# Routing attention and a squared-ReLU feed-forward on one core: narrow sums everywhere, last sums behind five products, one more pair turned by transfers, two heads in one load

## The chip, the cores and the metric

The kernel runs on one core of a Trainium2 chip. The metric is the device time of one execution in microseconds; the kernel before takes 984.49 us (median of 3 runs, 984.35 to 984.61). The profile shown is that of one execution with a span of 983.0 us.

The engines are called as in the profile: PE is TensorE (matmuls; PEld its weight loads), DVE is VectorE, ACT is ScalarE, POOL is GpSimd, SP is SyncE, whose queue (SPq) issues nearly all transfers here. L707 means line 707 of the kernel before.

## The reference

Four batches, eight heads, 768 rows of 64 numbers, 16 centroids per head; then a feed-forward on 3072 rows, 512 to 2048 to 512.

```python
q_assign = argmax(q_n @ c_n.T)          # cluster of each query, likewise k_assign
mask = q_assign[:, :, :, None] == k_assign[:, :, None, :]
scores = scale * np.matmul(q, k.transpose(0, 1, 3, 2))
scores = np.where(mask, scores, -1000000000.0)
attn = np.exp(scores - max)
attn = attn / (np.sum(attn, axis=-1, keepdims=True) + 1e-09)
out = np.matmul(attn, v)
# heads side by side: x is (3072, 512)
h = x @ w_in;  r = np.maximum(h, 0.0);  y = (r * r) @ w_out
```

So a key counts for a query only where both have the same nearest centroid; every query's weights are divided by their sum; and the result goes through two matrices with a squared ReLU in between.

## The kernel before

**Tiling.** The work goes by pairs of heads: pair = 4 * batch + hp, 16 pairs in all. The 768 queries of a pair are taken in two halves (h = 0, 1) of 384 columns (TB), the keys in six chunks of 128, two chunks at a time. One unit is (pair, h, c) with c = 0, 2, 4: 96 units. Batch 0 has its own order: units 0 to 11 are the first halves of pairs 0 to 3, units 12 to 23 their second halves. From unit 24 on (pairs 4 to 15) a pair does both halves, six units.

**A unit.** `scores` (L439) makes the products keys x queries into two PSUM tiles of two banks, ScalarE takes the exponential (L466). In batch 0 the mask is a second product of one-hot codes (`ohT`, bf16) added in PSUM; from batch 1 on VectorE multiplies with the mask instead (L470). `times_v` (L502) multiplies with v and accumulates in `av`. The exponentials also have to be summed over the keys. For the first halves of batch 0 (`first_half`) TensorE does it, by products with a tile of constants (`ups`), one for every unit, accumulated in `sm`. For all others GpSimd adds the exponentials up in `acc` (L480, L482), and a few products at the end of the half (L540) sum `acc` over the partitions.

**Sums.** `ones_products` (L486) has two forms. The narrow one writes 32 rows for 192 columns in each of four column groups; its result holds each sum once for a block of 32 rows. The reciprocal (L551) is then written to DRAM (`far_r`) and read back, repeated over 64 rows for each head (`rb`, L558). The wide form, used for pair 3's first half alone (`wide`, L498), writes 64 rows for 384 columns, so that the reciprocal (L545) is at once in the place of `rb`. `finish` (L567, profile line L570) multiplies `av` with `rb` into `xT`, the input of the feed-forward. Every reciprocal row also goes to `seen`, which is checked at the end.

**Before the scores.** Queries and keys must be turned, head dimension on the partitions. `load_qk` (L101) loads a pair, one transfer for each head of q and of k, into tiles where the two heads lie side by side (256 bytes each). For batch 0 `turn` (L249) transposes on TensorE, three parts of four, and ScalarE copies each part out (L258). For pairs 4 to 15 `split_words` (L269) copies the halves of each number apart on ScalarE (`flat`, L277, held by `issue_after` behind the last exponential traced), writes them to DRAM (`words`, L278), and `turn_words` (L286) reads them back with a transposing transfer (L288). Then come `logits` (L296, products with the centroids), `route` (L309: transposes L317, the argmax on VectorE L340 to L349) and the one-hot codes (`turn_onehot`, L363) or their spread (L394). `prep` (L409) lists these steps for a pair, and the main loop takes up to three of the list in each unit.

**Feed-forward.** The two halves of batch 0 are done plainly (`ffn`, L579: products L584 and L597), drawn in small portions between the units as filling for TensorE: `share` (L849 to L854) spreads the columns that are left over the units to come, RESERVE keeps three products of 512 columns for after the loop. A half enters the filling when `ends` (L784) has finished its last pair. The other three batches are done after the loop by `ffn_pair` (L610), which saves one product in eight (lines L676 and L707 in the profile).

**Weights.** In the first units 32 weight tiles are loaded (L139, four ahead), and each is rounded in six steps on ScalarE (L150, L152), VectorE (L155, L159, L162) and GpSimd (L166), four tiles in three units.

**Order.** The source is traced unit by unit. A scheduler then gives every engine its list: among the instructions that it reckons ready it takes the one traced first, where `high_priority` moves a block forward and `issue_after` holds one back. On the chip each engine works its list in order, and so does SyncE's queue. The loop delays things by hand: `complete` and `late` (L812 to L818) say in which unit `add_up` (L529) is traced after the last `times_v` of a half, `added` when `finish` follows.

Of the kernel before, what the change touches and what calls it, by code (L numbers as in the profile page):

```python
# [8 lines left out]
F32 = mybir.dt.float32  # L9
# [9 lines left out]
P = 128  # L19
# [6 lines left out]
def kernel(  # L26
# [74 lines left out]
    def load_qk(pair):  # L101
        if pair >= NG:
            return
        b, hp = divmod(pair, HP)
        raw[pair] = []
        for name, src in (("q_raw", q), ("k_raw", k)):
            t = loads.tile([P, NCH, 2 * D], F32, name=name, tag="qk")
            for e in range(2):
                (nc.scalar if pair == 0 and e else nc.sync).dma_start(
                    t[:, :, D * e : D * (e + 1)],  # L110
                    src[b, 2 * hp + e].rearrange("(p j) d -> p j d", p=P),
                )
            raw[pair].append(t)
# [135 lines left out]
    def turn(pair, part):  # L249
        if part == 0:  # L250
            pool = qkt_early if 2 <= pair < HP else qktp
            qkT[pair] = pool.tile([P, 2 * NCH, P], F32, name="qkT")
        pt = bank("pt", [P, 4, P])
        for i in range(4):
            which, c = divmod(4 * part + i, NCH)
            nc.tensor.transpose(out=pt[:, i], in_=raw[pair][which][:, c], identity=ident)
        dst = qkT[pair][:, 4 * part : 4 * part + 4]
        nc.scalar.copy(out=dst, in_=pt)  # L258
        if part == 2:
            raw.pop(pair)  # L260
            if pair in (0, 1, HP - 2):
                load_qk(pair + 2)


# [4 lines left out]
    def split_words(pair, which):  # L269
        if which == 0:  # L270
            words[pair] = dram.tile([2 * NCH, P, 2, 2 * D], U16, name="words")
        flat = loads.tile([P, NCH, 2, 2 * D], U16, name="flat", tag="qk")
        src = raw[pair][which].bitcast(U16).rearrange("p c (d two) -> p c two d", two=2)
        half = NCH // 2
        with tc.issue_after(last_exp[0]):
            for cols in (slice(0, half), slice(half, NCH)):
                nc.scalar.copy(out=flat[:, cols], in_=src[:, cols])  # L277
        nc.sync.dma_start(  # L278
            words[pair][NCH * which : NCH * (which + 1)].rearrange("c p two d -> p c two d"),
            flat,  # L280
        )
        if which == 1:
            raw.pop(pair)
            load_qk(pair + 1)

    def turn_words(pair):  # L286
        qkT[pair] = qktp.tile([P, 2 * NCH, P], F32, name="qkT")
        nc.sync.dma_start(  # L288
            qkT[pair].rearrange("p c n -> p (c n)").bitcast(U16),
            words.pop(pair).rearrange("c p two d -> (c p two) d"), transpose=True,  # L290
        )
# [17 lines left out]
    def route(pair):  # L309
        with tc.high_priority(offset=2000) if pair <= HP else ExitStack():  # L310
            number(pair)
# [95 lines left out]
        )  # L407

    def prep(pair):  # L409
        if pair < HP:  # L410
            return [
                lambda: turn(pair, 0), lambda: turn(pair, 1), lambda: turn(pair, 2),
                lambda: logits(pair), lambda: route(pair),
                lambda: turn_onehot(pair, 0), lambda: turn_onehot(pair, 1),
            ]

        split = [lambda i=i: split_words(pair + 1, i) for i in range(2 if pair + 1 < NG else 0)]
        first, second = split or (None, None)
        return [
            lambda: turn_words(pair), None, None, first, None, None,  # L420
            lambda: logits(pair), None, lambda: route(pair), second, None, None,
            None, None, lambda: spread(pair),
        ]
# [59 lines left out]
                out=acc[pair, h], in0=acc[pair, h], in1=t[:, 2 * i : 2 * i + 2], op=ALU.add  # L483
            )

    def ones_products(sm, wide, e, rhs, first, last):  # L486

        n = TB if wide else TB // 2
        rows = P * n // (2 * TB)
        return [  # L490
            dict(
                out=sm[rows * r : rows * (r + 1)], lhsT=ups[:, 0:rows],
                rhs=rhs[:, n * i : n * (i + 1)], start=first, stop=last,
            )
            for i, r in enumerate(range(e * P // (2 * rows), (e + 1) * P // (2 * rows)))
        ]

    def wide(pair, h):  # L498

        return (pair, h) == (HP - 1, 0)  # L500

    def times_v(pair, h, c):  # L502
        if c == 0:
            av[pair, h] = ps_av.tile([P, TB], F32, name="av", tag="av")
            if first_half(pair, h):
                n = TB if wide(pair, h) else TB // 2
                sums[pair, h] = ps_av.tile([P, n], F32, name="sm", tag="av")
        t = ex.pop((pair, h, c))
        products = [
            dict(  # L510
                out=av[pair, h][D * e : D * (e + 1)], lhsT=raw_v[pair][:, e, c + i],
                rhs=t[:, 2 * i + e], start=(c + i == 0), stop=(c + i == NCH - 1),
            )
            for i in range(2) for e in range(2)
        ]
        if first_half(pair, h):
            for i in range(2):
                one = [
                    ones_products(
                        sums[pair, h], wide(pair, h), e, t[:, 2 * i + e], c + i == 0, c + i == NCH - 1  # L520
                    )
                    for e in range(2)
                ]
                products += [p for both in zip(*one) for p in both]
        together(products, 4000)
# [3 lines left out]
    def add_up(pair, h):  # L529


        b, hp = divmod(pair, HP)
        if first_half(pair, h):
            sm = sums.pop((pair, h))
            if not wide(pair, h):
                nc.scalar.copy(out=xT_of(b, h)[:, hp], in_=av.pop((pair, h)))
        else:
            total = acc.pop((pair, h))
            sm = bank("sm", [P, TB // 2])
            one = [ones_products(sm, False, e, total[:, e], True, True) for e in range(2)]  # L540
            together([p for both in zip(*one) for p in both])
        row = 4 * (2 * pair + h)
        if wide(pair, h):
            rb = rbp.tile([P, TB], F32, name="rb")
            nc.vector.reciprocal(out=rb, in_=sm)  # L545
            nc.sync.dma_start(
                seen[row : row + 4], rb.rearrange("(e p) (g n) -> e p g n", e=2, g=2)[:, 0]
            )
        else:
            r = once.tile([P, TB // 2], F32, name="r")  # L550
            nc.vector.reciprocal(out=r, in_=sm)  # L551
            r = r.rearrange("(r p) n -> r p n", r=4)[:, 0]
            far = dram.tile([2, TB], F32, name="far_r")
            nc.sync.dma_start(far.rearrange("e (g n) -> (e g) n", g=2), r)
            nc.sync.dma_start(seen[row : row + 4], r)
            rb = rbp.tile([P, TB], F32, name="rb")
            for e in range(2):
                nc.sync.dma_start(rb[D * e : D * (e + 1)], far[e].partition_broadcast(D))  # L558
        spread_out[pair, h] = rb

    def xT_of(b, h):
        if (b, h) not in xT:
            pool = {0: xtp, 1: xt_first, 2 * B - 1: xtp}.get(2 * b + h) or later["xT"]
            xT[b, h] = pool.tile([P, KT, TB], F32, name="xT")
        return xT[b, h]
# [218 lines left out]
    def ends(halves):  # L784
        for pair, h in halves:
            b, hp = divmod(pair, HP)
            finish(pair, h)
            if hp == HP - 1 and (b, h) in PLAIN:
                fill.append(ffn(b, h))

    for u in range(len(units) + 2):
        if u < len(units):
            pair, h, c = units[u]
            if (p := next_pair(u)) is not None:
# [18 lines left out]
        while v_next < min(ready, len(units)):  # L813
            pair, h, c = units[v_next]
            times_v(pair, h, c)
            v_next += 1
            if c == NCH - 2:
                (late if u < HP * NCH and h else complete).append((pair, h))  # L818
        for pair, h in complete:
            with tc.high_priority(offset=1000) if first_half(pair, h) else ExitStack():  # L820
                add_up(pair, h)
            if h == 1:
                for d in (qkT, ids, qid):
                    d.pop(pair)
            if h == 1 or pair < HP:
                raw_v.pop(pair)
            if wide(pair, h):
                with tc.high_priority(offset=1000):
                    ends([(pair, h)])
            else:  # L830
                added.append((pair, h))

        rounding += 4
        while rounding >= 3:
# [263 lines left out]
```

## Time and profile before

| what | us |
|---|---|
| median time | 984.49 |
| span of the profiled execution | 983.0 |
| TensorE busy | 962.6 (98%) |
| VectorE busy | 562.4 (57%) |
| GpSimd busy | 376.9 (38%) |
| ScalarE busy | 315.4 (32%) |
| attention with plain feed-forward between | 0 to 543 |
| paired feed-forward (L676, L707) | 543 to 983 |
| scores and av products with their masks (L91, L94) | the greater part of 0 to 543 |
| plain feed-forward products L584 and L597 | 91.8 and 92.7 |

A line of the order in time reads: start in us, duration in us, engine, line and operation, what is written from what, shapes, how many; in brackets the idle time of the engine ahead of it and what ended it. In the chain of waits a line has start, duration and what the chain followed. A line of waits reads: who waited for whom, us in total, times, longest us. A line of SPq shows how long SyncE took to issue a transfer, not how long the transfer took.

### The profile page before, as it was taken

What the parts mean: (1) busy time and instruction counts of PE and PEld (TensorE: products, weight loads), DVE (VectorE), ACT (ScalarE), POOL (GpSimd) and SP (SyncE); (2) the same over time, 40 slices, a digit from 0 to 9 for tenths busy, and PEclk for the clock granted to TensorE, in tenths of its full rate; (3) what the DMA queues carried; (4) which work ended last, traced back from release to release, by engine and by line L of the source; (5) the groups of instructions that cost most, each with busy time, mean ns of one, the idle gap of its engine ahead of it and who ended that gap; (6) DMA issues with size and microseconds to landing.
All of it is one profiled execution on the core that took longest, in us unless ns stands there. A gap on an engine that the chain in (4) does not pass through costs nothing.

```text
span 983.0 us, 12011 instructions
## 1 busy us (share of the span) xinstructions
PE 962.6 (98%) x4455; PEld 552.8 (56%) x4455; DVE 562.4 (57%) x913; ACT 315.4 (32%) x510; POOL 376.9 (38%) x277
## 2 busy tenths in 40 slices
PE   7999989999999999999999999999999999999997
PEld 4544444443344444443343555888556888556886
DVE  5777778766566665667654865532566531656331
ACT  5886755444445545544231111000111000111000
POOL 1336666655656556565666231002231002231000
PEclk9999999999999999999999999999999999999999
DMA  9666572534546345452310000000000000000000
GB/s 248 199 186 177 164 212 76 136 108 106 135 111 156 98 109 123 111 142 75 74 42 16 15 0 1 11 22 22 11 1 1 21 22 22 1 0 1 22 22 24
DMA packets 127575, 74.32 MB, mean 76 GB/s; under 512 B 90906, under 2 KB 118934, under 8 KB 127510
## 3 DMA queue, kind: packets, MB, share of 16 engines
q1 hardware_dynamic: 125798, 73.06, 28.1%
q8 instruction: 37, 0.61, 0.3%
q10 hardware_dynamic: 1712, 0.43, 0.2%
q14 instruction: 28, 0.23, 0.1%
HBM read 48.07 MB, written 15.86 MB: 65 GB/s over the span
## 4 chain that ended last, share of the span: by engine, by line
PE 81%; DVE 6%; DMA 5%; issue 3%; ACT 1%; POOL 1%; SPq 1%; ACTq 0%; DVEq 0%; POOLq 0%
PE bank L707 22%; PE bank L676 22%; PE po L597 7%; PE ph L584 6%; PE sc L91 6%; PE sc L94 5%; PE av L91 5%; PE av L94 4%; DMA rb<-far_r 3%; DVE w_raw L162 1%; DVE r L551 1%; PE sm L91 1%; DVE ex L470 1%; DMA far_r<-r 1%; POOL w_in L166 1%
## 5 line engine op out<-in xcount | busy, mean ns | idle before, releaser
L482 POOL TENSOR_TENSOR acc<-acc,ex 128x768 f32<-128x768 f32 x112 | 207.1, 1849 | 115.0 <-DVE ex L470 98.4
L470 DVE SCALAR_TENSOR_TENSOR ex<-qid,ids,sc 128x384 f32<-128x384 bf16 x288 | 157.7, 608 | 63.3 <-ACT sc L466 45.6
L466 ACT ACTIVATE sc<-sc 128x768 f32<-128x768 f32 x144 | 108.5, 792 | 162.1 <-PE sc L94 144.6
L94 PE MATMUL sc<-qkT 64*128 64x384 f32 x576 | 153.4, 505 | 0.7
L94 PE MATMUL av<-ex,v_raw 128*64 128x384 f32 x576 | 136.9, 495 | 0.0
L665 POOL TENSOR_TENSOR w_s<-w_in 128x256 f32<-128x256 f32 x24 | 18.3, 762 | 279.9 <-PE bank L707 162.0
L646 DVE TENSOR_TENSOR g<-bank,g 128x384 f32<-128x384 f32 x144 | 77.9, 556 | 81.5 <-PE bank L676 80.5
L707 PE MATMUL bank<-w_out,g 128*128 128x256 f32 x432 | 95.2, 379 | 0.0
L584 PE MATMUL ph<-xT,w_in 128*128 128x384 f32 x256 | 91.8, 498 | 3.3 <-DVE best L341 2.3
L597 PE MATMUL po<-w_out,gT 128*128 128x512 f32 x192 | 92.7, 615 | 0.0
L91 PE MATMUL sc<-qkT 64*128 64x384 f32 x192 | 87.9, 538 | 2.6 <-DVE ex L470 2.6
L707 PEld LDWEIGHTS bank<-w_out,g 128*128 128x128 f32 x432 | 82.1, 190 | 11.8
L646 DVE TENSOR_TENSOR osb<-bank,osb 128x256 f32<-128x256 f32 x54 | 22.1, 423 | 107.6 <-PE bank L707 102.2
L94 PEld LDWEIGHTS sc<-qkT 64*128 64x128 f32 x576 | 65.4, 187 | 28.6 <-issue 6.7
L91 PE MATMUL av<-ex,v_raw 128*64 128x384 f32 x192 | 81.0, 504 | 0.0
L676 PE MATMUL bank<-xT,w_in 128*128 128x384 f32 x192 | 69.9, 487 | 0.0
L676 PE MATMUL bank<-x_t,w_s 128*128 128x384 f32 x192 | 69.8, 486 | 0.0
L676 PE MATMUL bank<-xT,w_s 128*128 128x384 f32 x192 | 69.8, 486 | 0.0
L584 PEld LDWEIGHTS ph<-xT,w_in 128*128 128x128 f32 x256 | 45.6, 189 | 42.7 <-issue 16.0
L94 PEld LDWEIGHTS av<-ex,v_raw 128*64 128x64 f32 x576 | 49.8, 137 | 34.6 <-issue 34.4
L480 POOL TENSOR_TENSOR acc<-ex 128x768 f32<-128x768 f32 x28 | 51.0, 1822 | 46.9 <-DVE ex L470 39.0
L707 PE MATMUL bank<-w_t,g_s 128*128 128x256 f32 x288 | 65.1, 379 | 0.0
(128 smaller groups left out, 1222.8 us busy)
## 6 DMA issues: line engine op xcount, KB each, us to landing
words<-flat SPq DMA_DIRECT2D x24, 384.0 KB
w_raw<-in_moe_w_in_dram SPq DMA_DIRECT2D x16, 512.0 KB
w_raw<-in_moe_w_out_dram SPq DMA_DIRECT2D x16, 512.0 KB
v_raw<-in_v_dram SPq DMA_DIRECT2D x20, 384.0 KB
q_raw<-in_q_dram SPq DMA_DIRECT2D x31, 192.0 KB
k_raw<-in_k_dram SPq DMA_DIRECT2D x31, 192.0 KB
rb<-far_r SPq DMA_DIRECT2D x62, 96.0 KB
out_dram<-osb SPq DMA_DIRECT2D x23, 256.0 KB
```

The source lines that it names most:

```text
L91: last = nc.tensor.matmul(**next(products))
L94: last = nc.tensor.matmul(**product)
L466: last_exp[0] = nc.scalar.activation(out=t[:, 2 * i : 2 * i + 2] if pair < HP else src, in_=src, func=ACT.Exp, scale=SCALE).ins
L470: nc.vector.scalar_tensor_tensor(out=t[:, 2 * i + e], in0=qid[pair][1][:, h, e], scalar=ids[pair][:, ch % NB, 2 + ch // NB, e : e + 1], in ...
L480: nc.gpsimd.tensor_tensor(out=acc[pair, h], in0=t[:, 0:2], in1=t[:, 2:4], op=ALU.add)
L482: nc.gpsimd.tensor_tensor(out=acc[pair, h], in0=acc[pair, h], in1=t[:, 2 * i : 2 * i + 2], op=ALU.add)
L584: nc.tensor.matmul(ph, lhsT=w_in[:, kk, f * P : (f + 1) * P], rhs=xT[b, h][:, kk], start=(kk == 0), stop=(kk == KT - 1),)
L597: nc.tensor.matmul(po, lhsT=gT[f][:, i * P : (i + 1) * P], rhs=w_out[:, f], start=(f == 0), stop=(f == FT - 1),)
L646: nc.vector.tensor_tensor(out=out, in0=bank, in1=to, op=ALU.add)
L665: nc.gpsimd.tensor_tensor(out=s1, in0=a[1][0], in1=a[1][1], op=ALU.add)
L676: nc.tensor.matmul(bank, lhsT=operands[j][0][:, kk], rhs=operands[j][1][:, kk], start=(kk == 0), stop=(kk == H2 - 1),)
L707: nc.tensor.matmul(bank, lhsT=operands[j][0][:, f], rhs=operands[j][1][:, f], start=(f == 0), stop=(f == F2 - 1),)
```

## The change

Four edits, in one diff.

- **Narrow sums everywhere.** The wide form goes. Pair 3's first half is summed like the others, its `av` is copied to `xT` by ScalarE, and the reciprocals go through DRAM. `finish` for it is now traced one unit later, with high priority. The transfer to `seen` is traced behind the two that read `rb`.
- **Last sums later.** The sums of the last half (pair 15, h = 1) join `late`: they are traced one unit after the last value products, with a portion of filling between. The loop has one more round for that.
- **Pair 3 turned by transfers.** `split_words` for pair 3 comes in among pair 2's preparation, and pair 3's preparation begins with `turn_words`, with logits in the next unit.
- **Two heads in one load.** From pair 3 on, q and k of both heads come in one transfer each, in tiles with the heads one after the other, 1536 bytes in one piece. `split_words` takes the heads apart instead of the two halves of the chunks.

```diff
@@ load_qk @@
         for name, src in (("q_raw", q), ("k_raw", k)):
+            if pair > HP - 2:
+                t = loads.tile([P, 2, NCH, D], F32, name=name, tag="qk")
+                heads = src[b, 2 * hp : 2 * hp + 2]
+                nc.sync.dma_start(t, heads.rearrange("h (p j) d -> p h j d", p=P))
+                raw[pair].append(t)
+                continue
@@ turn @@
-            if pair in (0, 1, HP - 2):
+            if pair < 2:
                 load_qk(pair + 2)
@@ split_words @@
-        src = raw[pair][which].bitcast(U16).rearrange("p c (d two) -> p c two d", two=2)
-        half = NCH // 2
+        src = raw[pair][which].bitcast(U16).rearrange("p e c (d two) -> p e c two d", two=2)
         with tc.issue_after(last_exp[0]):
-            for cols in (slice(0, half), slice(half, NCH)):
-                nc.scalar.copy(out=flat[:, cols], in_=src[:, cols])
+            for e in range(2):
+                nc.scalar.copy(out=flat[:, :, :, D * e : D * (e + 1)], in_=src[:, e])
@@ turn_words @@
-        qkT[pair] = qktp.tile([P, 2 * NCH, P], F32, name="qkT")
+        pool = qkt_early if pair < HP else qktp
+        qkT[pair] = pool.tile([P, 2 * NCH, P], F32, name="qkT")
@@ prep @@
-        if pair < HP:
-            return [
-                lambda: turn(pair, 0), lambda: turn(pair, 1), lambda: turn(pair, 2),
-                lambda: logits(pair), lambda: route(pair),
-                lambda: turn_onehot(pair, 0), lambda: turn_onehot(pair, 1),
-            ]
         split = [lambda i=i: split_words(pair + 1, i) for i in range(2 if pair + 1 < NG else 0)]
         first, second = split or (None, None)
+        onehot = [lambda: turn_onehot(pair, 0), lambda: turn_onehot(pair, 1)]
+        turned = [lambda: logits(pair), lambda: route(pair)]
+        if pair < HP - 1:
+            turned = [lambda i=i: turn(pair, i) for i in range(3)] + turned
+            return turned + ([first, *onehot, second] if pair == HP - 2 else onehot)
+        if pair < HP:
+            return [lambda: turn_words(pair), None, None, *turned, *onehot]
@@ ones_products, wide, times_v: the wide form is taken out @@
-        n = TB if wide else TB // 2
-        rows = P * n // (2 * TB)
+        n, rows = TB // 2, P // 4
...
-    def wide(pair, h):
-        return (pair, h) == (HP - 1, 0)
...
@@ add_up @@
-            if not wide(pair, h):
-                nc.scalar.copy(out=xT_of(b, h)[:, hp], in_=av.pop((pair, h)))
+            nc.scalar.copy(out=xT_of(b, h)[:, hp], in_=av.pop((pair, h)))
...
-        if wide(pair, h):
-            rb = rbp.tile([P, TB], F32, name="rb")
-            nc.vector.reciprocal(out=rb, in_=sm)
-            nc.sync.dma_start(
-                seen[row : row + 4], rb.rearrange("(e p) (g n) -> e p g n", e=2, g=2)[:, 0]
-            )
-        else:
...
-            nc.sync.dma_start(seen[row : row + 4], r)
             rb = rbp.tile([P, TB], F32, name="rb")
             for e in range(2):
                 nc.sync.dma_start(rb[D * e : D * (e + 1)], far[e].partition_broadcast(D))
+        nc.sync.dma_start(seen[row : row + 4], r)
@@ ends and the main loop @@
-            finish(pair, h)
+            with tc.high_priority(offset=1000) if (pair, h) == (HP - 1, 0) else ExitStack():
+                finish(pair, h)
...
-    for u in range(len(units) + 2):
+    for u in range(len(units) + 3):
...
-                (late if u < HP * NCH and h else complete).append((pair, h))
+                (late if h and not HP * NCH <= u < len(units) else complete).append((pair, h))
...
-            if wide(pair, h):
-                with tc.high_priority(offset=1000):
-                    ends([(pair, h)])
-            else:
-                added.append((pair, h))
+            added.append((pair, h))
```

## The prediction

> **What bounds the kernel now.** I read the engine totals first, then the busy time of each engine by stage, then the order of instructions on TensorE and on SyncE in the two stages that the change touches.
>
> ```profile
> PE 962.6 (98%) x4455; PEld 552.8 (56%) x4455; DVE 562.4 (57%) x913; ACT 315.4 (32%) x510; POOL 376.9 (38%) x277
> ```
>
> and, from the busy times by stage (stretch, its length, then busy us of TensorE, its weight loads, VectorE, ScalarE, GpSimd, the granted clock, the transfers' share, GB/s):
>
> ```profile
> 543.00:983.00 440.00, 434.39 (x1682) 318.78 (x1680) 209.80 (x353) 40.25 (x82) 68.39 (x88) 1.00 0.03 12
> ```
>
> TensorE is busy 98% of the span, so time is TensorE work plus its holes. The second block is the last stage, the paired feed-forward: 440 us that no edit touches. Everything here is decided in the first 543 us.
>
> The first place is the end of attention. The chain of waits, 526 to 545 us:
>
> ```profile
> 530.82 1.81 POOL acc L482
> 532.71 1.81 POOL acc L482
> 534.57 0.53 PE sm L91
> 535.43 7.36 PE po L597 x14
> ```
>
> and the stretches there:
>
> ```profile
> 532.00:535.00 3.00, 0.67 (x10) 0.20 (x8) 0.00 (x0) 0.00 (x0) 2.92 (x3) 0.89 0.00 0
> 535.00:538.00 3.00, 3.00 (x12) 1.26 (x5) 1.36 (x1) 0.00 (x0) 3.00 (x6) 0.54 0.01 3
> ```
>
> The reader sees the last sum products waiting for GpSimd's running sum while 14 ready products of L597 stand behind them in TensorE's order. The wait list has this as 2.3 us, and the clock falls afterwards.
>
> The second place is batch 0, the order on TensorE from 48 us:
>
> ```profile
> 48.37 0.87 PE L256 MATMUL pt<-ident,q_raw 128*128 128x128 f32 x6
> 49.08 0.38 PE L256 MATMUL pt<-ident,k_raw 128*128 128x128 f32 x2
> 51.21 0.66 PE L256 MATMUL pt<-ident,k_raw 128*128 128x128 f32 x4
> 53.24 0.51 PE L91 MATMUL lg<-qkT,cnT 128*32 128x384 f32 x1
> 58.23 2.16 PE L94 MATMUL sm<-ex,ups 128*32 128x192 f32 x48
> 62.49 0.49 PE L94 MATMUL sc<-ohT 64*128 64x384 bf16 x4
> 70.77 4.04 PE L94 MATMUL sm<-ex,ups 128*64 128x384 f32 x24
> 82.29 1.53 PE L584 MATMUL ph<-xT,w_in 128*128 128x384 f32 x4 [0.81 <-DVE xT L570]
> ```
>
> These are pair 3's turns, its logits, pair 2's narrow sums, pair 3's mask products, pair 3's wide sums, and the first feed-forward products, which wait 0.81 us for pair 3's scaled output. In 45 to 61 us TensorE is busy 15.80 of 16.00, ScalarE 12.88.
>
> The path that pair 3 is to take exists already for pairs 4 to 15, on SyncE's queue:
>
> ```profile
> 133.22 0.39 SPq L278 DMA_DIRECT2D words<-flat  x1
> 138.09 3.39 SPq L288 DMA_TRANSPOSE qkT<-words  x1
> ```
>
> and in the list of SyncE's waits:
>
> ```profile
> SPq L288 <- DMA words<-flat: 1.7, 1, 1.7
> ```
>
> The write of k's words lands 4.9 us after its issue: the transposing transfer, next in order, waited for it.
>
> **What the Trainium skill says.** (1) "TensorE: Matmul & The Clock Gate", section "What's actually happening": the array drops to half clock after an idle window of about 3.4 us and needs about as long to recover. Here 0.54 of the clock was granted in 535 to 538 us, after a hole of only 2.3 us, so a shorter hole can cost as well. (2) "TensorEngine Tiling (Array Packing)", "Theoretical Speedup": outputs of at most 64 columns pack two tiles, of at most 32 four. The trace agrees: the wide sums take from 70.77 to the next product at 74.73, 3.96 us; the narrow ones from 58.23 to 60.32, 2.09 us, for the same sums. (3) "DMA: Bandwidth & Descriptors", "Latency and other measured facts": a transposing transfer runs at 261 GB/s on one kernel. That page alone would give, as an estimate, 3.0 us for the 786 KB of a pair. (4) The same page, "Specifications": transfers under 512 B do not reach line rate. 90906 of 127575 packets are under 512 B, but the transfer engines are busy only 28.1%, so no run here shows that this limits anything.
>
> **The change part by part.**
>
> Turning by transfers. It removes 12 transposes from TensorE: 48.37 to 49.40 is 1.03 us, 51.21 to 51.80 is 0.59 us, together 1.62 us, and three ScalarE copies of L258, 3 x 0.59 = 1.8 us. It adds four flat copies on ScalarE, 4 x 0.835 = 3.3 us, two writes and one transposing transfer. The q copies stand behind the exponentials of unit 4; ScalarE has a hole of 1.71 us at 39.1 to 40.8 us, which takes their 1.67 us. The k copies stand behind unit 5's (40.81 to 42.2 us); four rounding activations are ahead of them to about 44.7 us and the two mask copies of pair 2 compete with them (44.89 to 46.4 us). So k is flat at about 47.7 us, and I charge 0.5 us for an exponential pushed back. SyncE is then free (before, it waited with a weight load for GpSimd until 46.8 us). The words land 4.9 us later, at 52.6 us. The transposing transfer: its landing is not shown by any wait. From below it is its median issue of 4.43 us; from above, 15.3 us (issued at 101.69 us, read without waiting at 116.96 us). I take 4.43 plus the 2 us that a 3 KB write of r needs from issue until the next transfer starts behind it (204.12 to 205.73 us), so 6.4 us. Queries and keys are turned at about **59 us, against 53.2 us now**.
>
> Who waits? The logits, behind them the route on VectorE, the one-hot turn, and unit 9's scores. From logits to mask products the work is 0.8 + 0.5 (L307) + 0.55 (L317) + 3.0 (five VectorE steps, 56.43 to 59.49 us) + 0.84 + 1.5 on ScalarE = 7.2 us, 7.7 with handovers; so mask products at about 66.7 us against 62.5 us. Work that can be pulled ahead: unit 8's value products, 1.44 us, and the scores of unit 9 themselves. From 59 to 67.8 us, when unit 9's first exponential frees a bank, TensorE has 0.75 + 1.4 + 0.5 + 0.84 + 0.42 = 3.9 us of work. That leaves a hole of 4.9 us in pieces, shorter by whatever TensorE is late itself. I take 4.0 us, and 0.5 us for the clock. Bounds: nothing, if k is flattened right at 42.2 us and the transfer takes the page's 3 us; 7 us plus a full 1.7 us of half clock if the words meet the weight loads on SyncE.
>
> Narrow sums for pair 3. 3.96 - 2.09 = 1.9 us less on TensorE; VectorE's reciprocal falls from 2.54 (L545) to 1.35 us. It adds the round trip through DRAM: r, far_r, two rb, about 9 us. In its shadow TensorE has units 12, 13 and 14, since the first feed-forward now enters the list at unit 13 and is first drawn on at unit 14: 10 products of L584 move from unit 12 to later. Their work stays, but the 0.81 us wait goes. I charge nothing for the round trip.
>
> Last sums later. Five L597 products, 5 x 0.43 = 2.1 us, go ahead of the sums; the hole shrinks from 2.33 to about 0.2 us. The clock: 3 x 0.11 + 3 x 0.46 = 1.7 us come back. Together 3.8 us. What is behind the sums (r, far_r, rb, xT L570) starts no later, since GpSimd ends at 534.5 us anyway; the first copy of the next stage waits for it, but eight banks of products cover that.
>
> One load for two heads. SyncE's two issues of about 0.6 us become one of 0.4 us (as v_raw L118), and packets grow from 256 B. Off the path, save where VectorE waits for rb ahead of ex (longest wait 6.2 us) and TensorE for ex, 2.6 us in three waits. I credit 0.5 us of 2.6. Moving the seen transfer behind rb: nothing, rb waits for far_r meanwhile.
>
> **Sum:** 1.6 + 1.9 + 0.8 + 3.8 + 0.5 = 8.6 us gained, 5.0 us lost (0.5 + 4.0 + 0.5): 3.6 us less. 984.5 - 3.6 is about **981.0 us**, the forecast, chance 0.50.
>
> **The rivals.**
> - The transfer is hidden: words and transpose arrive by about 56 us. Then some 1 us is lost, -7.6 us, **977 us**. For it: ScalarE has 3 us free in 45 to 61 us, and the load of pair 3 is long there. Against: the k copies can't leave before unit 5's exponentials, and 4.9 + 4.4 us are measured. Chance 0.22.
> - The new wait swallows it: the words are caught behind weight loads (SyncE waited 11.7 us for GpSimd in 40 to 60 us, in five waits), the hole is 7 us or more, the clock halves, and the blocked SyncE holds up weight loads that ScalarE's rounding waits for ahead of the exponentials: 11 to 12 us lost against 8.6 gained, +3 us, **987.5 us, slower**. Against: the weights are loaded four tiles ahead. Chance 0.13.
> - VectorE becomes the limit after 80 us: with ten products fewer in units 12 and 13, TensorE meets VectorE's rounding work earlier (VectorE busy 19.21 of 20.00 in 90 to 110 us), and the existing wait of 2.3 us of L584 for L341 near 130 us grows by about 3 us: **984 us**, no change. Against: VectorE's own idle stretch before 87.6 us, 5.5 us behind ScalarE, shrinks too. Chance 0.15.
>
> **How the numbers follow.** The forecast spans 979 to 983.5 us by the bounds above. Below 982.5 us (faster by over 0.2%): all of the first rival and four fifths of the forecast, 0.62. Within 0.2%: the rest of the forecast and nearly all of the third rival, 0.24. Slower: 0.14. The range 976 to 986.5 us leaves out half of the second rival and the tails of the others.
>
> **What would show it.** Right: at the end of attention, L597 products between the last av and sm, no wait of sm for acc above 0.5 us, granted clock 1.0; no L256 products of pair 3; all sums of 192 columns; lg of pair 3 after 57 us with a wait on the transposing transfer, and a hole ahead of unit 9's mask products. Wrong: no hole there (then 977 us), lg after 62 us, VectorE waits growing near 130 us, or a start of the paired feed-forward that waits for xT.

## The result and the profile after

The changed kernel takes **989.7 us** (median of 6 runs, 988.99 to 994.49) against 984.55 us for the kernel before beside it: ratio 1.0062, interval 1.0042 to 1.0082. It is slower by 5 to 6 us (the ratio on record is not the quotient of the two medians, which is 1.0052; percentages below go by such ratios); the forecast was 981.0 us, within 976 to 986.5. Line numbers below are those of the changed kernel: L577 and L590 are the feed-forward products (L584 and L597 before), L283 the write of the words, L294 the transposing transfer, L544 the reciprocal, L547, L551 and L550 the transfers to far_r, to seen and to rb.

The totals of the page, to be laid beside the first line shown of before:

```profile
PE 965.1 (98%) x4467; PEld 552.4 (56%) x4467; DVE 563.9 (57%) x913; ACT 317.3 (32%) x512; POOL 375.7 (38%) x277
```

TensorE is busy for 965.1 us instead of 962.6 although 12 transposes and half of pair 3's sums are gone. A busy time grows without more work when products run at a lower clock: a value product takes 0.54 us at 53.9 us in this trace and 0.90 us at 66.7 us, in a stretch at half clock. So I looked for holes and for the granted clock. Busy times by stage for the changed kernel (columns as before: stretch, length, then TensorE, weight loads, VectorE, ScalarE, GpSimd, clock, share of transfers, GB/s):

```profile
57.00:61.00 4.00, 0.87 (x20) 0.26 (x12) 4.00 (x6) 0.79 (x2) 1.39 (x1) 1.00 1.11 214
61.00:69.00 8.00, 8.00 (x30) 3.09 (x23) 3.13 (x7) 0.48 (x1) 1.28 (x1) 0.57 0.72 257
...
107.00:116.00 9.00, 6.17 (x12) 3.30 (x11) 8.93 (x7) 4.76 (x9) 7.66 (x6) 0.62 0.95 249
...
549.50:989.50 440.00, 434.38 (x1682) 318.76 (x1680) 210.54 (x353) 40.19 (x82) 68.97 (x89) 1.00 0.04 12
```

and the first two stretches in the kernel before:

```profile
57.00:61.00 4.00, 4.00 (x68) 2.42 (x64) 3.84 (x8) 3.79 (x7) 0.92 (x2) 1.00 0.49 161
61.00:69.00 8.00, 8.00 (x51) 3.50 (x50) 6.23 (x8) 6.84 (x11) 3.96 (x3) 1.00 0.48 133
```

The last stage is what it was (434.38 of 440 us). Two places went wrong. From 57 to 61 us TensorE works 0.87 us of 4; from 61 to 69 us it is busy, but at 0.57 of its clock, and ScalarE has 0.48 us of work where it had 6.84. From 107 to 116 us the same happens again: a hole, then 0.62 of the clock.

The order on TensorE shows what the first place waited for:

```profile
60.61 0.51 PE L91 MATMUL lg<-qkT,cnT 128*32 128x384 f32 x1 [3.13 <-DMA qkT<-words]
...
71.06 0.50 PE L94 MATMUL sc<-ohT 64*128 64x384 bf16 x4
```

and SyncE's queue why it came so late (start, time of the issue, transfer):

```profile
45.48 0.34 SPq L145 DMA_DIRECT2D w_raw<-in_moe_w_in_dram  x1
47.30 0.53 SPq L547 DMA_DIRECT2D far_r<-r  x1
47.88 0.55 SPq L551 DMA_DIRECT2D seen<-r  x1
48.95 0.34 SPq L145 DMA_DIRECT2D w_raw<-in_moe_w_in_dram  x1
49.39 1.17 SPq L550 DMA_DIRECT2D rb<-far_r  x2
50.65 0.53 SPq L283 DMA_DIRECT2D words<-flat  x1
51.23 0.54 SPq L110 DMA_DIRECT2D k_raw<-in_k_dram  x1
52.37 0.34 SPq L145 DMA_DIRECT2D w_raw<-in_moe_w_in_dram  x1
54.99 3.49 SPq L294 DMA_TRANSPOSE qkT<-words  x1
```

The key words were flat on ScalarE at 45.48 us and left at 50.65 us: 5.2 us behind two weight loads, a reciprocal's round trip and its copy to seen. (The copy to seen is traced behind rb now, yet it still leaves ahead of it, at 47.88 against 49.39 us; this part of the edit changed nothing in the queue.) The transposing transfer left at 54.99 us and had landed 5.6 us later. The logits start at 60.61 us (53.24 before), the mask products of unit 9 at 71.06 us (62.49 before).

The second place, on VectorE and TensorE:

```profile
106.35 2.30 DVE L168 SCALAR_TENSOR_TENSOR w_raw<-w_raw 128x512 uint32<-128x512 uint32 x1
108.58 1.34 DVE L544 RECIPROCAL r<-sm 128x192 f32<-128x192 f32 x1
```

```profile
109.98 8.39 PE L577 MATMUL ph<-xT,w_in 128*128 128x384 f32 x16 [2.83 <-DVE r L544]
```

VectorE is rounding weights here, almost without a pause (6.97 of 7 us in 100 to 107; 6.52 before), and the reciprocal whose bank the products of L577 wait for stands behind that. The rounding is late because its first step, on ScalarE, stood still behind unit 9's exponentials from 57.8 to 72.9 us: GpSimd's last step of a weight tile was followed by the next one 12.5 us after. A late rounding does not make this hole by itself, as the transfers alone show further down.

At the end of attention the chain of waits reads as forecast:

```profile
540.51 1.81 POOL acc L489
...
542.41 1.81 POOL acc L489
...
544.26 0.35 PE sm L91
```

and TensorE's order has plain products ahead of the sums:

```profile
541.86 1.98 PE L590 MATMUL po<-w_out,gT 128*128 128x512 f32 x4
544.26 0.35 PE L91 MATMUL sm<-acc,ups 128*32 128x192 f32 x1 [0.42 <-POOL acc L489]
```

The sums wait 0.42 us for acc (2.33 before) behind four plain products (the forecast had five), and the clock stays at 1.00 from 535 to 547 us.

**A sum over the whole execution.** I added up, in each profile, the idle time of TensorE between products and the time at half clock. Before: 13.4 us idle, 10.2 us at half clock (worth 5.1 us). After: 17.4 and 17.1 us (8.5 us). That is 4.0 + 3.4 = 7.4 us more lost, against a span that is 6.5 us longer; by this sum the rest shrank by 0.9 us. In all fourteen profiles of this study the span less both losses is 961 to 967 us, while the losses go from 14 to 30 us. So most of what sets these profiles apart is holes and what the clock does after them. The sum is no sharper than some 4.5 us: two profiles of one kernel, the one without the transfers, have 966.5 and 962.0 us.

One place in this sum does not belong to the change. Near 470 us products of scores wait for VectorE, which prepares the paired feed-forward; in the changed kernel this is the line

```profile
477.36 0.56 PE L91 MATMUL sc<-qkT 64*128 64x384 f32 x1 [2.43 <-DVE ex L477]
```

with 3.4 us of half clock behind it; in the kernel before the same wait is 0.87 us, with none. That makes 3.3 of the 7.4 us. But the kernel without the transfers has 2.47 us here in one profile and 0.85 us in the other, so it is a difference between executions.

### The profile page after: what moved, and what is told of

It reads as the page before. It is cut to its first block, busy times and chain, and to the rows that moved or that the text cites. A ratio compares the mean times of both kernels' runs of the same rounds, so it can differ in the third digit from the quotient of the medians.

```text
span 989.5 us, 12012 instructions
## 1 busy us (share of the span) xinstructions
PE 965.1 (98%) x4467; PEld 552.4 (56%) x4467; DVE 563.9 (57%) x913; ACT 317.3 (32%) x512; POOL 375.7 (38%) x277
## 4 chain that ended last, share of the span: by engine, by line
PE 82%; issue 6%; DVE 4%; DMA 3%; POOL 2%; SPq 1%; ACT 0%; POOLq 0%; DVEq 0%; ACTq 0%
PE bank L700 22%; PE bank L669 22%; PE po L590 8%; PE ph L577 7%; PE sc L91 6%; PE sc L94 5%; PE av L91 5%; PE av L94 5%; POOL w_in L172 2%; DMA rb<-far_r 2%; PE sm L91 1%; DVE ex L477 1%; PE lg L91 1%; DVE w_raw L168 1%; DMA far_r<-r 1%
## 5 line engine op out<-in xcount | busy, mean ns | idle before, releaser
L577 PE MATMUL ph<-xT,w_in 128*128 128x384 f32 x256 | 94.8, 512 | 4.1 <-DVE r L544 2.8
L590 PE MATMUL po<-w_out,gT 128*128 128x512 f32 x192 | 92.3, 612 | 0.0
L577 PEld LDWEIGHTS ph<-xT,w_in 128*128 128x128 f32 x256 | 47.0, 195 | 44.6 <-issue 14.5
L700 PE MATMUL bank<-w_t,g 128*128 128x256 f32 x288 | 65.1, 379 | 0.0
```

The source lines that it names most:

```text
L577: nc.tensor.matmul(ph, lhsT=w_in[:, kk, f * P : (f + 1) * P], rhs=xT[b, h][:, kk], start=(kk == 0), stop=(kk == KT - 1),)
L590: nc.tensor.matmul(po, lhsT=gT[f][:, i * P : (i + 1) * P], rhs=w_out[:, f], start=(f == 0), stop=(f == FT - 1),)
L700: nc.tensor.matmul(bank, lhsT=operands[j][0][:, f], rhs=operands[j][1][:, f], start=(f == 0), stop=(f == F2 - 1),)
```

## The experiments

All ratios are to the kernel before, run on the same chip (medians there 985.0 to 986.1 us).

**Without the transfers**

The changed kernel, pair 3 turned on TensorE as before:

```diff
-            if pair > HP - 2:
+            if pair > HP - 1:
...
+        if pair < HP:
+            return [
+                lambda: turn(pair, 0), lambda: turn(pair, 1), lambda: turn(pair, 2),
+                lambda: logits(pair), lambda: route(pair),
+                lambda: turn_onehot(pair, 0), lambda: turn_onehot(pair, 1),
+            ]
```

> The changed kernel with pair 3 of batch 0 turned on TensorE again; narrow sums, late last sums and the two-head loads (from pair 4 on) stay. If the late transposing transfer is the cause: the hole of 3.1 us ahead of pair 3's logits, its half clock and the hole of 2.8 us near 107 us go, 979 to 981 us, some 5 us faster than before. If the narrow sums of pair 3 are the cause: the hole of TensorE behind a reciprocal near 107 us stays and the time is 986 us or more.

Measured 981.28 us, ratio 0.9946 (0.9928 to 0.9964): this one edit undone, the change gains. The hole before the logits and the one near 107 us are gone; one of 3.98 us, which ends at 93.7 us, is new and is looked at below.

**Each part alone**

The last sums later alone (two lines of the main loop):

```diff
-    for u in range(len(units) + 2):
+    for u in range(len(units) + 3):
...
-                (late if u < HP * NCH and h else complete).append((pair, h))
+                (late if h and not HP * NCH <= u < len(units) else complete).append((pair, h))
```

> The kernel before with the last sums one unit later and nothing else. All theories: the hole of 2.3 us ahead of the last sums and the half clock behind it go, 980.5 to 981 us (-3.8 us).

Measured 982.81 us, 0.9975 (0.9964 to 0.9987), a smaller gain than expected. The wait list has the wait of the sums at 0.4 us.

The transfers for pair 3 with the load of two heads that they are written for, the rest as before:

```diff
-        qkT[pair] = qktp.tile([P, 2 * NCH, P], F32, name="qkT")
+        pool = qkt_early if pair < HP else qktp
+        qkT[pair] = pool.tile([P, 2 * NCH, P], F32, name="qkT")
...
+            return [lambda: turn_words(pair), None, None, *turned, *onehot]
```

> The kernel before with pair 3 turned by transfers (and the two-head load that this edit needs, from pair 3 on), wide sums and early last sums kept. If the transfer is the cause: a hole of about 3 us ahead of pair 3's logits, half clock behind it and a second hole after 100 us, 992 to 996 us. If the narrow sums are: 984 to 987 us.

Measured 991.15 us, 1.0048 (1.0035 to 1.0062), with a hole of 4.34 us before the logits and 10.2 us of half clock after it. The words left at 51.28 us, behind rb again. This edit alone makes the kernel slower. The second hole that I expected after 100 us did not come, although the rounding stood still even longer here (14.5 us on GpSimd). What there is, is the hole that the kernel before has near 129 us (2.28 us):

```profile
138.86 0.88 PE L591 MATMUL ph<-xT,w_in 128*128 128x384 f32 x2 [2.23 <-DVE best L347]
```

The narrow sums alone:

```diff
-    def wide(pair, h):
-        return (pair, h) == (HP - 1, 0)
...
-            if wide(pair, h):
-                with tc.high_priority(offset=1000):
-                    ends([(pair, h)])
-            else:
-                added.append((pair, h))
+            added.append((pair, h))
```

> The kernel before with narrow sums everywhere (with the later finish of pair 3 and the transfer to seen moved), pair 3 turned on TensorE, early last sums, loads as before. If the transfer is the cause of the loss: 981.5 to 983 us. If the narrow sums are: 988 to 991 us with TensorE waiting for VectorE's reciprocal near 107 us.

Measured 983.45 us, 0.9968 (0.996 to 0.9976). It gains, but the round trip is seen: the first products of the feed-forward wait 3.26 us for the scaled output of pair 3, where the kernel before waited 0.81 us. In exchange the hole of 2.3 us near 129 us shrinks to 0.72 us.

The load of two heads alone, from pair 4 on:

```diff
+            if pair > HP - 1:
+                t = loads.tile([P, 2, NCH, D], F32, name=name, tag="qk")
+                heads = src[b, 2 * hp : 2 * hp + 2]
+                nc.sync.dma_start(t, heads.rearrange("h (p j) d -> p h j d", p=P))
```

> The kernel before with only the load of two heads at once, from pair 4 on. Forecast: -0.5 us (0.05%). Rival 1 (SyncE's queue matters more than I credited): -1 to -2 us. Rival 2 (512-byte and larger pieces make the transfers no shorter, and nobody waits for these loads): no difference that can be measured, within 0.1%.

Measured 982.3 us, 0.9971 (0.996 to 0.9982): some 3 us, six times my credit. The page's packets, to be held against 127575 and 90906:

```profile
DMA packets 96470, 74.31 MB, mean 76 GB/s; under 512 B 53658, under 2 KB 87830, under 8 KB 96406
```

The transfers' share falls from 28.1% to 26.9%. Which wait it shortened is not clear: in the profile 0.9 us of idle TensorE and two stretches of half clock are missing, and the latter come and go from run to run.

**The whole again, and the words moved in the queue**

The next three ran beside the load. First the changed kernel as it is:

> The changed kernel once more, beside the kernel before on the same chip as the three that follow. Alone, the transfers cost 0.48% and the other parts together gained 0.54%, so if the parts simply add, the whole should be within 0.1% of the kernel before; the first measurement gave 0.6% slower. Theory (the late turn costs more once the narrow sums send one more round trip through SyncE's queue and once VectorE falls behind): 0.4 to 0.8% slower again. Rival (the first measurement met an unlucky chip): within 0.2% of the kernel before.

Measured 992.85 us, 1.0088 (1.0057 to 1.0118). The theory's case, and not the chip. (The sum in the expectation counts the load twice, since the transfers alone had it too; with 0.29% for it the parts add up to -0.09%, still far from +0.88%.) The hole before the logits was 5.10 us here, and 10.2 us of half clock followed.

Then the words of pair 3's keys ahead in SyncE's order:

```diff
+        with tc.high_priority(offset=1000) if pair < HP else ExitStack():
-        nc.sync.dma_start(
+            nc.sync.dma_start(
                 words[pair][NCH * which : NCH * (which + 1)].rearrange("c p two d -> c p two d"),
```

> The changed kernel with one thing other: the write of pair 3's key words stands ahead of the reciprocals' write, a weight load and the two broadcasts on SyncE's queue instead of behind them. Theory (those words waited 5.2 us in the queue, from 45.5 to 50.7 us, and everything that was lost follows from it): words issued near 45.7 us, transposing transfer issued by 52 us, logits of pair 3 near 57.5 us, the hole of 3.1 us before them under 0.7 us, no half clock from 61 to 68 us, and 5 to 8 us less than the changed kernel. Rival (the transfer's own landing, or ScalarE's copies and the route behind the logits, set it): the logits stay after 60 us, or the hole moves to unit 9's scores and stays above 2.5 us; time within 2 us of the changed kernel.

Measured 990.81 us, 1.0066 (1.0044 to 1.0087): my theory, as I had put it, failed. The logits stayed after 60 us, as the rival had it, and the time is 2 us below the changed kernel's beside it. SyncE's queue in this kernel:

```profile
47.34 0.34 SPq L145 DMA_DIRECT2D w_raw<-in_moe_w_in_dram  x1
47.78 0.38 SPq L284 DMA_DIRECT2D words<-flat  x1
...
52.24 1.14 SPq L551 DMA_DIRECT2D rb<-far_r  x2
53.43 0.57 SPq L110 DMA_DIRECT2D k_raw<-in_k_dram  x1
54.10 0.42 SPq L145 DMA_DIRECT2D w_raw<-in_moe_w_in_dram  x1
54.58 5.57 SPq L295 DMA_TRANSPOSE qkT<-words  x1
```

The words left 3 to 4 us earlier, but the transposing transfer did not: between the two stand rb, which waits for its reciprocals to come back, a load of keys and a weight load. It left at 54.58 us, landed 7.7 us later, and the hole was 3.81 us. Two transfers in a row each wait behind other work; moving one leaves the other.

Words from ScalarE's queue:

```diff
-        nc.sync.dma_start(
+        (nc.scalar if pair < HP else nc.sync).dma_start(
             words[pair][NCH * which : NCH * (which + 1)].rearrange("c p two d -> p c two d"),
```

> The changed kernel with pair 3's words (queries and keys) written from ScalarE's queue, so that they wait for nothing on SyncE; two issues of some 0.5 us each are added to ScalarE. Theory: as with the words first in SyncE's queue, or somewhat better as the transposing transfer also stands ahead of one weight load: logits near 57 us, no half clock there, 5 to 8 us less than the changed kernel. Rival (the queue is not the cause): hole of 2.5 us or more stays, time within 2 us of the changed kernel, or ScalarE's two issues push unit 6's exponentials back and it costs as much as it gives.

Measured 991.46 us, 1.0076 (1.0052 to 1.0101). The words left at 45.57 us and the transposing transfer at 52.36 us, behind rb and the load of keys; the logits start at 58.74 us, 2 us earlier than in the changed kernel. Yet the hole is 4.72 us, because the scheduler now put the logits ahead of unit 8's value products and sums in TensorE's list, so that TensorE reached them at 54.02 us.

**Both moved, and both early**

The transposing transfer with high priority too, the words on ScalarE's queue:

```diff
+        with tc.high_priority(offset=1000) if pair < HP else ExitStack():
-        nc.sync.dma_start(
+            nc.sync.dma_start(
                 qkT[pair].rearrange("p c n -> p (c n)").bitcast(U16),
```

> The changed kernel with pair 3's words written from ScalarE's queue, and the transposing transfer ahead of one broadcast, the load of keys and a weight load in SyncE's order. With the words alone moved, the transposing transfer still stood behind these and landed no earlier (58.7 to 62.3 us). Theory (what counts is when the transposing transfer is issued): issued near 51 us instead of 52.4 to 55.7, landed 6 to 7.5 us later, so logits at 57 to 58 us; a hole of 2 to 4 us remains, since TensorE's fixed order reaches the logits at 54 us; time 1 to 4 us below the changed kernel. Rival (the landing is not what counts): hole and time as with the words alone moved, within 1 us.

Measured 993.97 us, 1.0079 (1.0049 to 1.0109): a miss. The scheduler put it between the two transfers to rb, the first of which had to wait for far_r, so it left at 53.01 us, not 51, and the hole was 4.1 us. The time is that of the words alone moved (1.0076), as the rival had it; but the transposing transfer left no earlier than there (52.36 us), so the order of the queue was not changed enough to test what I meant to test.

So I moved the beginning instead: the words of pair 3 are flattened behind pair 1's one-hots. A fifth load buffer is needed for it, and the weights are staged three ahead to make room.

```diff
-    AHEAD = 4
+    AHEAD = 3
...
-    loads = ctx.enter_context(tc.tile_pool(name="loads", bufs=4))
+    loads = ctx.enter_context(tc.tile_pool(name="loads", bufs=5))
...
-            return turned + ([first, *onehot, second] if pair == HP - 2 else onehot)
+            early_split = [lambda i=i: split_words(HP - 1, i) for i in range(2)]
+            return turned + onehot + (early_split if pair == 1 else [])
```

> The changed kernel with pair 3's words flattened and written some 12 us earlier, behind pair 1's one-hots. That needs a fifth load buffer, for which the weights are staged three tiles ahead instead of four. Theory (the queries and keys of pair 3 came too late: words, then the transposing transfer, each behind other transfers in SyncE's order, and hole and half clock follow from that): the transposing transfer is issued before 48 us, logits of pair 3 by 55 us with no wait on a transfer, no half clock from 60 to 75 us, no ScalarE hole of over 3 us there, VectorE not behind, and so no hole of L577 near 112 us; time 8 to 14 us below the changed kernel, level with or 1 to 2 us below the kernel whose pair 3 is turned on TensorE. Rival 1 (the narrow sums' round trip and VectorE's rounding lose the time, not the landing): the hole near 60 us goes but holes of over 4 us in all stay between 85 and 140 us, and the time is within 5 us of the changed kernel. Rival 2 (three tiles ahead are too few, rounding waits for weights): ScalarE and VectorE wait for weight loads, time above the kernel before.

Measured 983.8 us, **0.9972** (0.9955 to 0.9989), 1.15% below the changed kernel's 1.0088 on this chip. SyncE's queue and TensorE's order:

```profile
30.15 0.43 SPq L283 DMA_DIRECT2D words<-flat  x1
...
35.81 0.53 SPq L283 DMA_DIRECT2D words<-flat  x1
...
40.51 6.55 SPq L294 DMA_TRANSPOSE qkT<-words  x1
```

```profile
52.70 0.51 PE L91 MATMUL lg<-qkT,cnT 128*32 128x384 f32 x1
...
56.66 0.55 PE L323 MATMUL lt<-ident,lgs 128*128 128x128 f32 x3 [1.75 <-ACT lgs L313]
```

The logits wait for no transfer, and the clock stays at full speed from 18 to 472 us. With the words early the loss is gone, so the late landing was what cost. (The two side edits, a fifth buffer and three tiles ahead, were not run alone.) It is not the whole gain: the kernel without the transfers is 0.3% faster still, by the ratios. ScalarE waited 2.5 us for a weight load here, up to 51.96 us (three ahead are fewer than four), which pushed its next exponentials and the copy of the logits back, and so the transposes of L323 by 1.75 us; and there are two holes of 2.1 us before feed-forward products, near 87 and 111 us. My theory had none near 112 us, and rival 1 had over 4 us of them between 85 and 140 us, which came, though not its time. The second of them waits for ScalarE (gT); the wait for the reciprocal, 2.83 us in the changed kernel, is 0.60 us.

**What the narrow sums are worth beside the others**

The kernel without the transfers, once more:

> The changed kernel with pair 3 turned on TensorE, once more, for the comparison on one chip with the two others. Before: 0.54% below the kernel before. If late sums (-0.25%), narrow sums (-0.32%) and the load for two heads (-0.29%) added up, it would be 0.86% below. Theory (the narrow sums' round trip leaves a hole near 90 us and takes part of the gain back): again 0.4 to 0.7% below. Rival (they add): 0.8 to 0.9% below, and the first value was a chance of the half clock.

Measured 980.47 us, 0.9939 (0.9918 to 0.996): as the theory had it, though the interval just reaches the rival. The hole on TensorE, then VectorE:

```profile
88.30 4.87 PE L576 MATMUL ph<-xT,w_in 128*128 128x384 f32 x10 [4.36 <-DVE xT L562]
```

```profile
77.08 1.34 DVE L543 RECIPROCAL r<-sm 128x192 f32<-128x192 f32 x1
...
86.21 1.94 DVE L562 SCALAR_TENSOR_TENSOR xT<-xT,rb 128x384 f32<-128x384 f32 x1 [3.51 <-ACT w_raw L158]
```

The bracket of the last line names a rounding step of ScalarE, which the scaling does not read; it reads rb, issued at 81.63 and 82.18 us, and for the same step in the changed kernel the profile names rb<-far_r. From the start of the reciprocal to the end of the scaling it takes 11 us, and TensorE's other work lasts to 83.94 us.

Last, the late sums and the load without the narrow sums and without the transfers (the diffs of the two parts above together):

> The kernel before with the last sums behind five plain products and the load for two heads, so the changed kernel without the transfers and without the narrow sums of pair 3. Against the one without the transfers alone (-0.54 and -0.61%) it shows what the narrow sums are worth beside the others. If the parts add: -0.25 and -0.29%, together -0.54%, and the narrow sums would be worth nothing here though alone they gave -0.32%. Theory (their gain of 1.9 us is eaten by the hole of 4 us that the round trip of the reciprocals leaves before the first products of L577 near 88 us): -0.5 to -0.7%, level with that kernel, no hole over 1 us between 80 and 95 us, but one of some 2.3 us near 128 us. Rival (the narrow sums gain there as they do alone): -0.2 to -0.35%.

Measured 979.85 us, **0.9930** (0.9908 to 0.9953), on another chip. The gain is the same without the narrow sums, within the intervals. In place of the hole of 4.4 us there is one of 1.60 us at 81.5 us (I had expected none over 1 us) and the one of 2.23 us near 129 us, as before the change. Both this kernel and the one without the transfers beat both kernels of the study; which is the better one is not settled.

## Why the prediction was wrong

**The step that failed** is the first, "Turning by transfers": the wait of the words in SyncE's queue, and above all the clock and the rounding behind it. The sentence "SyncE is then free (before, it waited with a weight load for GpSimd until 46.8 us)" took the queue of before for the queue of after. The words were to leave at 47.7 us; they left at 50.65 us, and the transposing transfer, which I let go at their landing at 52.6 us, left at 54.99 us. The landing itself was well guessed: 6.4 us against 5.6 us here, 7.4 and 7.7 us in two other runs (the sum took 2 us for what its lines, 204.12 to 205.73, show as 1.6). Queries and keys were turned at 60.6 us instead of 59. That is only 1.6 us late, and the hole of 3.1 us is even less than the 4.0 us I allowed. What was mis-sized is what the hole set off. I gave 0.5 us for the clock; two windows at half clock cost 3.4 us, and in the second profile of this kernel three cost 5.1 us. At half clock the way from the logits to the mask products took 10.4 us instead of 7.7: VectorE had the one-hots at 66.8 us, but their turn on TensorE stood behind scores and value products until 68.9 us. And I named, for the second rival, that the rounding of weights would be held up, but put nothing for it into the forecast: a second hole of 2.83 us came and, with 6.8 us at half clock, another 3.4 us. The two places together lost 3.1 + 3.4 + 2.8 + 3.4 = 12.7 us, of which I had 5. The second place is not the transfers' alone: with them but without the narrow and the late sums there was no hole near 107 us, and without the transfers there was none either. It takes the late turn together with one of the other edits; that this is the narrow sums is likely and not shown.

**The rivals.** What happened is the second rival, "The new wait swallows it", in mechanism (words behind weight loads, half clock, rounding held up) and nearly in size: 987.5 us against 989.7, a loss of 11 to 12 us against 12.7. That the sizes agree is partly luck, since its hole was to be 7 us or more and was 3.1 us. I gave it 0.13, because "the weights are loaded four tiles ahead". This says how early a load is issued, not what stands ahead in SyncE's order; the weight loads wait for buffers (one left at 45.48 us after 2.8 us without an issue), and so does everything behind them. What the third rival named, products that wait for a VectorE behind with its rounding, came too, near 110 us. The spread of the forecast, "979 to 983.5 us by the bounds above", was narrower than these bounds, which give 976.4 to 985.1 us; even they left 989.7 us out.

**Narrow sums.** The saving was right: pair 3's sums take 0.79 + 1.44 = 2.2 us against 3.96 us, 1.7 us saved for 1.9 predicted. "I charge nothing for the round trip" was wrong: in the kernels without the transfers it costs a hole of 3.3 to 4.4 us where 0.8 us was. Alone the narrow sums still gain 0.32%, some 3 us, of which the profile shows a part: 1.7 us of sums, and 1.6 us at the hole near 129 us, less 2.5 us of the round trip's hole; where the rest comes from stays open. Beside the late sums and the load nothing of the gain is seen, within the intervals. In the changed kernel the round trip's hole is 0.60 us, since pair 3 is late there by other means.

**Last sums later.** Right in place and mechanism: the wait is 0.42 us (0.2 predicted), no half clock. Alone 2.5 us (0.25%), for 3.8 predicted. The half clock at this place, 1.7 us of my sum, is not there in every run: in three other profiles with the wait of 2.3 us unchanged (the transfers, the narrow sums and the load alone) no half clock followed it.

**One load.** 0.5 us was forecast, some 3 us came. I had credited only the waits that the trace tied to these loads, and the share of the transfers. The packets are fewer by a quarter in the whole; which transfer got faster was not found.

**Sum.** The late sums, the narrow sums and the load measured one by one (0.25, 0.32 and 0.29%) give 8.5 us, against 7.0 predicted for them (3.8, 1.9 + 0.8 and 0.5). Together they give 5.3 to 6.0 us. The transfers alone take 0.77% (1.0048 with the load, 0.9971 for it), but 1.2 to 1.5% on top of the other three. For this the profiles offer the second hole: with the transfers alone the feed-forward products waited 2.2 us near 137 us, as before near 129; in the changed kernel they wait 0.7 us there, but 2.8 us already at 107 us, and two windows of half clock follow. Why it moved there was not taken apart further; the reciprocals' longer way is one candidate.

## What to carry to other kernels

A transfer on a busy in-order queue costs its own time plus the wait of whatever stands ahead, once for every transfer of its chain: write down the queue's order with the new transfers in it before giving a landing time, and do not take a gap in the old trace for a free queue. Here the words stood 5.2 us in the queue. If data comes too late, start its chain earlier; moving one link did nothing here. A hole on TensorE of 3 us or more should be charged with the half clock after it: in the nine such holes of these profiles hole and clock together came to 1.4 to 2.3 times the hole. The producers that starve meanwhile (here ScalarE, then the rounding on three engines) can open a second hole, as in the changed kernel.

## What the runs showed that I had not expected

- Every one of the nine holes on TensorE of over 3 us brought half clock, which began between 1.2 us before its end and 4 us after it; of 30 holes of 2 to 3 us 17 did, of 38 holes of 1 to 2 us 4, all of them the same hole at 14 us. All 30 stretches at half clock stand behind one of these holes, the time after TensorE's last product left out. The stretches at half clock are 3.41, 6.83 or 10.24 us, that is one, two or three of the same length. The same kernel differs in this from run to run (the changed kernel 17.1 and 20.5 us in two profiles), which is a part of the spread of its times, 988.74 to 998.36 us. "TensorE: Matmul & The Clock Gate", section "What's actually happening", gives about 3.4 us for the window; this agrees with the length of the stretches, while as the shortest hole that costs it would be too long for these traces.
- A transposing transfer of the same 786 KB landed 5.6 to 7.7 us after its issue.
- A transfer put ahead changed the order of another engine: the scheduler, reckoning with the earlier data, moved the logits forward on TensorE, and the hole grew (4.72 us) though the data came 2 us earlier.
